# The first 4 KB of each row of w1 in loads of 2 to 32 rows

## The chip, the core and the metric

The kernel runs on one NeuronCore of a Trainium2 chip; the other seven are idle. The metric is the device time of one execution in microseconds (us), as the median of several runs. Five engines work side by side: PE (TensorE, the matrix multiplications), DVE (VectorE), ACT (ScalarE), POOL (GpSimd) and SP (SyncE, which here does nothing but start transfers). They meet at semaphores only. Transfers between the memory (HBM) and the on-chip buffer (SBUF, 128 partitions, called rows below) are carried by 16 DMA engines. An instruction on SP or ACT issues a transfer, and the profile counts the transfers of each issuer as one queue. A transfer raises a semaphore by 16 in all once its data has arrived.

## The reference

One token goes through a parallel block: the sum of the input, attention over a cache of 65536 positions, and a small MLP. All numbers are 32-bit floats.

```python
xn = layernorm(x)                                   # x: 512 numbers
q  = (xn @ wq) as 32 heads of 128                   # wq: 512 x 4096
k, v: 8 heads of 65536 x 128, each used by 4 query heads
scores = einsum("bhqd,bhkd->bhqk", q, k) * 128 ** -0.5
o  = einsum("bhqk,bhkd->bhqd", softmax(scores), v)
attention = o (32 * 128 numbers) @ wo               # wo: 4096 x 512
mlp = relu(xn @ w1) @ w2                            # w1: 512 x 1792, w2: 1792 x 512
y  = x + attention + mlp                            # 512 numbers
```

The keys and the values are 256 MiB each; wq and wo are 8 MiB each, w1 and w2 3.5 MiB each. So 561 MB have to come in, and 2 KB go out.

## The kernel before

**Stages.** SBUF has two large tiles, `kt` and `vt`, of 128 rows by 16384 numbers (64 KB of each row, 8 MiB in all), and a tile `wt` of 128 rows by 7168 numbers (28 KB of each row, 3.5 MiB). First `wq` comes into `kt` in three loads (of 16, 16 and 32 KB of each row), then `w1` into `wt` in one load. Then come the cache's pieces in turn: 32 loads of keys into `kt` and 32 of values into `vt`, each of 128 rows with 64 KB, alternating. At the end `wo` comes into `kt` in three loads and `w2` into `wt` in five, of 12, 8, 4, 2 and 2 KB of each row (`W2_CUTS`). All of these loads are issued by SP, on one queue.

**What sets the order.** Everything is written out by hand. SP issues the three loads of wq and that of w1 with nothing in their way. A load of keys waits for the semaphore `kfree`, that is, until the scores of the keys before have left `kt` and their largest has been found; a load of values waits for `vfree`, until PE has multiplied the values before. So at most one load is in flight and one more queued behind it.

**What the engines do.** For each piece of keys PE computes scores against four queries (L313), DVE transposes them (L366) and finds the largest, ACT takes the exponentials (L256), and PE multiplies them with the values (L292). Between the two, PE runs matrix multiplications over the MLP's first layer, three times over (`PASSES`, L281); the first of them waits for the semaphore `sum`.

**The use of w1.** POOL waits until all of w1 is in (L217), multiplies its four parts of 1792 numbers by the normed input (L219) and adds the four up (L222 to L224). The last addition raises `sum`. `wt` is next written when w2 comes at the very end.

**The end.** SP issues w2's five loads once POOL has the MLP's hidden layer (L226). PE multiplies each part of w2 as it arrives (L331, then L339 for the last three loads), DVE transposes the sum (L417), and SP stores the result (L179).

Of the kernel before, what the change touches and what calls it, by code (L numbers as in the profile page):

```python
# [12 lines left out]
P = 128  # L13
D = 512
# [15 lines left out]
FB = DFF_ALL // P  # L30
# [13 lines left out]
W2_CUTS = [6, 4, 2, 1, 1]  # L44
W2_SUM = 12
W2_ROWS = 10
PASSES = 3


def take(e, sem, n=1):  # L50

    return e.sem_inc(sem, -n).wait_op(sem, n, "sem-ge")  # L52
# [7 lines left out]
def attention_and_mlp_kernel(  # L60
# [12 lines left out]
    sp, pe, dve, act, pool = nc.sync, nc.tensor, nc.vector, nc.scalar, nc.gpsimd  # L73
    scale = float(DH) ** -0.5

    def sbuf(name, *shape):
        return nc.alloc_sbuf_tensor(name, list(shape), F32).ap()
# [3 lines left out]
    def sem(name):  # L81
        if name not in sems:
            sems[name] = nc.alloc_semaphore(name)
        return sems[name]
# [7 lines left out]
    wt = sbuf("wt", P, FB * D)  # L92
# [47 lines left out]
    w1_row = w1.rearrange("p a f -> p (a f)")  # L140
# [16 lines left out]
    for i in range(1, len(WQ_CUTS)):  # L157
        cut = slice(wq_at[i], wq_at[i + 1])
        sp.dma_start(kt[:, cut], wq_row[:, cut]).then_inc(sem(WQ_SEMS[i]), 16)  # L159
    sp.dma_start(wt, w1_row).then_inc(sem("w1"), 16)  # L160
    take(sp, sem("kfree"))
    sp.dma_start(kt, k[0, 0]).then_inc(sem("k"), 16)
    with sp.Fori(0, NCH - 1) as n:
# [7 lines left out]
    for i in range(len(WO_CUTS)):  # L171
        cut = slice(wo_at[i] * D, wo_at[i + 1] * D)
        sp.dma_start(kt[:, cut], wo_row[:, cut]).then_inc(sem(f"wo{i}" if i else "k"), 16)
    sp.wait_ge(sem("hT"), 1)
    for i in range(len(W2_CUTS)):
        cut = slice(w2_at[i] * D, w2_at[i + 1] * D)
# [37 lines left out]
    after(pool.tensor_copy(qpad[:, :XA], xn), "pool", chain[0]).then_inc(sem("q"), 1)  # L214
    f = DFF_ALL
    w1_of = [wt[:, a * f : (a + 1) * f] for a in range(XA)]
    pool.wait_ge(sem("w1"), 16)  # L217
    for a in range(XA):
        last = pool.tensor_scalar_mul(w1_of[a], w1_of[a], xn[:, a : a + 1])  # L219
    last.then_inc(sem("pool"), 1)  # L220
# [50 lines left out]
    with nc.body("turns", valid_engines=[pe.engine]):  # L271
# [3 lines left out]
        with pe.If(t > 1):  # L275
            after(pe.transpose(pma[:GROUP, :P], m, ident), "d2p").then_inc(sem("p2d"), 1)  # L276
            after(pe.matmul(pmb[:, :GROUP], ones[:GROUP, :], dg, start=True, stop=True), "d2p", 2).then_inc(sem("p2d"), 1)  # L277

            with pe.Fori(0, PASSES):
                for c in range(CT):  # L280
# [8 lines left out]
            for i in range(n):  # L289
                c = 32 * (i % CT)  # L290
                b = i * WIDE
# [32 lines left out]

    for b in range(W2_ROWS):
        if b == w2_at[1]:
# [4 lines left out]
        last = pe.matmul(  # L331
            y4[c : c + 1, :], hT[:, b : b + 1], wt[:, b * D : (b + 1) * D], start=(b < CT), stop=(b >= W2_ROWS - CT)
        )
        if b in w2_at:
            after(last, f"w2{w2_at.index(b)}", 16)
    last.then_inc(sem("p2d"), 1)
    for b in range(W2_ROWS, FB):
        for c in range(CT):
            last = pe.matmul(  # L339
                yacc[32 * c : 32 * c + 1, :], hT[:, b : b + 1], wt[:, b * D + c * P : b * D + (c + 1) * P],  # L340
                start=(b == W2_ROWS), stop=(b == FB - 1),
            )
# [113 lines left out]
```

## Time and profile before

| what | value |
|---|---|
| time, median of 3 runs | 1303.13 us (1302.83 to 1303.29) |
| span of the profiled execution | 1301.3 us |
| bytes moved | 561.02 MB, 431 GB/s over the span |
| share of the 16 DMA engines taken by SP's queue | 99.7% |
| PE busy | 774.9 us (60%) |
| DVE busy | 274.8 us (21%) |
| ACT busy, POOL busy | 76.2 us, 34.8 us |
| w1's load, issue to landing | 28.9 us |

The span reaches from the first to the last instruction of the profiled execution; it is the only time that this execution has. The runs that were timed lie 1.8 us above it. A row of the timeline has the start in us, the duration in us, the engine with the line of the kernel, the operation with what it writes and reads, and in brackets how long the engine was idle before it and what ended that. SPq is a DMA being issued by SP, PEld a weight load of PE. A row of a table by stretches has the stretch, its length, the busy time of each engine with its instructions, the clock granted to TensorE, the busy share of the DMA engines and the rate.

### The profile page before, as it was taken

The numbers are of one execution on the slowest core, as the hardware profiler recorded it, in microseconds if no ns is written. First come the engines' busy times: TensorE is split into PE (matmuls) and PEld (weight loads), VectorE is DVE, ScalarE is ACT, GpSimd is POOL, SyncE is SP. The second block draws the span as 40 slices with busy tenths as digits, with TensorE's granted clock in tenths as the row PEclk, the third lists the DMA queues.
The fourth block names the chain that finished last, engine by engine and source line by source line (L and its number), as shares of the span: only waits on it lengthen the run. The fifth ranks groups of instructions, "written<-read, shape, count | busy, mean of one in ns | idle before, by whom it ended". The sixth has DMA issues, their size and how long they took to land.

```text
span 1301.3 us, 13055 instructions
## 1 busy us (share of the span) xinstructions
PE 774.9 (60%) x5474; PEld 231.1 (18%) x5474; DVE 274.8 (21%) x466; ACT 76.2 (6%) x299; POOL 34.8 (3%) x30
## 2 busy tenths in 40 slices
PE   3365674665576456566555566666567466557557
PEld 1111121111121111121111121111112111112112
DVE  2211222211222220222220122221122221122222
ACT  1000000000000000000000000000000000000000
POOL 1900000000000000000000000000000000000000
PEclk9677877776887777786776777677777777777779
DMA  9999999999999999999999999999999999999998
GB/s 403 451 419 451 419 451 419 435 435 419 451 419 451 419 451 419 449 421 423 447 419 451 419 451 419 451 419 435 435 419 451 419 451 419 451 419 443 427 420 370
DMA packets 11236, 561.02 MB, mean 431 GB/s; under 512 B 1505, under 2 KB 1505, under 8 KB 1890
## 3 DMA queue, kind: packets, MB, share of 16 engines
q1 hardware_dynamic: 11088, 561.00, 99.7%
q10 hardware_dynamic: 146, 0.00, 0.0%
q8 instruction: 1, 0.02, 0.0%
q14 instruction: 1, 0.01, 0.0%
HBM read 560.99 MB, written 0.00 MB: 431 GB/s over the span
## 4 chain that ended last, share of the span: by engine, by line
issue 94%; DMA 3%; POOL 2%; SPq 0%; PE 0%; DVE 0%; POOLq 0%
DMA wt<-w 3%; POOL wt L219 1%; POOL wt L224 0%; POOL wt L222 0%; POOL wt L223 0%; SPq L177 0%; SPq L159 0%; PE banks L339 0%; DVE ysb L417 0%; SPq L151 0%; POOL hT L226 0%; SPq L452 0%; POOLq L156 0%
## 5 line engine op out<-in xcount | busy, mean ns | idle before, releaser
L313 PE MATMUL banks<-kt,qpad 128*32 128x512 f32 x2176 | 310.0, 733 | 311.1 <-PEq L52 308.7
L292 PE MATMUL banks<-vt,probs 128*16 128x512 f32 x2048 | 271.3, 690 | 82.1 <-PEq L52 82.1
L366 DVE STREAM_TRANSPOSE tr<-banks 128x1024 f32<-128x1024 f32 x136 | 170.0, 1250 | 471.4 <-PE banks L313 466.8
L313 PEld LDWEIGHTS banks<-kt,qpad 128*32 128x32 f32 x2176 | 84.5, 131 | 509.6 <-issue 496.3
L281 PE MATMUL banks<-wt,ones 128*1 128x448 f32 x768 | 121.3, 786 | 0.0
L292 PEld LDWEIGHTS banks<-vt,probs 128*16 128x16 f32 x2048 | 68.4, 108 | 298.4 <-issue 298.4
L392 DVE COPY o_sb<-banks 128x512 f32<-128x512 f32 x32 | 22.1, 692 | 455.3 <-PE banks L292 455.3
L254 ACT ACTIVATE corr<-diff 128x8 f32<-128x8 f32 x32 | 6.7, 208 | 1179.8 <-ACTq L52 1179.8
L256 ACT ACTIVATE probs<-tr,nb_new 128x128 f32<-128x128 f32 x128 | 65.3, 521 | 0.0
L276 PE MATMUL banks<-ident,m 128*4 128x128 f32 x32 | 9.7, 303 | 78.9 <-DVE m L384 78.9
L302 PE MATMUL banks<-sel,o_sb 128*128 128x4 f32 x256 | 32.8, 252 | 18.7 <-PEq L52 18.7
L302 PEld LDWEIGHTS banks<-sel,o_sb 128*128 128x128 f32 x256 | 31.0, 191 | 20.6 <-issue 20.6
L226 POOL TENSOR_SCALAR hT<-ysum 128x14 f32<-128x14 f32 x1 | 0.3, 257 | 1220.7 <-DVE ysum L404 1220.7
L384 DVE TENSOR_REDUCE m<-tr 128x4 f32<-128x512 f32 x32 | 32.2, 1006 | 2.9
L281 PEld LDWEIGHTS banks<-wt,ones 128*1 128x1 f32 x768 | 20.2, 100 | 58.9 <-issue 58.4
L277 PE MATMUL banks<-dg,ones 4*128 4x4 f32 x64 | 15.4, 309 | 20.0 <-DVE dg L387 20.0
L256 ACT ACTIVATION_READ_ACCUMULATOR probs<-tr,nb_new 128x1 f32 x128 | 24.0, 187 | 0.0
L276 PEld LDWEIGHTS banks<-ident,m 128*4 128x4 f32 x32 | 2.6, 81 | 108.0 <-DVE m L384 108.0
L219 POOL TENSOR_SCALAR wt<-wt,xn 128x1792 f32<-128x1792 f32 x4 | 19.1, 4797 | 16.5 <-DMA wt<-w 16.5
L277 PEld LDWEIGHTS banks<-dg,ones 4*128 4x128 f32 x64 | 12.6, 245 | 27.1 <-DVE dg L387 27.1
L299 PEld LDWEIGHTS banks<-part_sum,ones 128*128 128x128 f32 x64 | 9.5, 188 | 27.2 <-issue 27.2
L395 DVE TENSOR_TENSOR lo_run<-lo_run,banks 128x8 f32<-128x8 f32 x32 | 5.2, 163 | 40.0 <-DVEq L52 40.0
(69 smaller groups left out, 91.1 us busy)
## 6 DMA issues: line engine op xcount, KB each, us to landing
kt<-wq SPq DMA_DIRECT2D x2, 2048.0 KB, 9.3
kt<-wq SPq DMA_DIRECT2D x1, 4096.0 KB, 20.8
kt<-wo SPq DMA_DIRECT2D x1, 4096.0 KB, 15.5
kt<-wo SPq DMA_DIRECT2D x2, 2048.0 KB, 22.2
wt<-w SPq DMA_DIRECT2D x1, 3584.0 KB, 28.9
wt<-w SPq DMA_DIRECT2D x1, 1536.0 KB, 9.5
wt<-w SPq DMA_DIRECT2D x1, 1024.0 KB, 11.7
kt<-k SPq DMA_DIRECT2D x32, 24.1
```

Of the source, the lines that this page charges most:

```text
L219: last = pool.tensor_scalar_mul(w1_of[a], w1_of[a], xn[:, a : a + 1])
L256: last = act.activation(probs[:, :, g], tr[:, :, g], AF.Exp, bias=nb_new[:, g : g + 1], scale=scale, accum_out=part_sum[:, g : g + 1],)
L276: after(pe.transpose(pma[:GROUP, :P], m, ident), "d2p").then_inc(sem("p2d"), 1)
L277: after(pe.matmul(pmb[:, :GROUP], ones[:GROUP, :], dg, start=True, stop=True), "d2p", 2).then_inc(sem("p2d"), 1)
L281: ins = pe.matmul(hrow[32 * c : 32 * c + 1, :], ones[:, :1], hb[:, :, 32 * c : 32 * c + 32], start=True, stop=True,)
L292: last = pe.matmul(acc[c : c + WIDE * GROUP, :], probs[:, b : b + WIDE, :].rearrange("p b g -> p (b g)"), vt[:, b * DH : (b + WIDE) * DH], ...
L299: pe.matmul(lo_new[:, 0, :], ones, part_sum, start=True, stop=True).then_inc(sem("vfree"), 1)
L302: last = pe.matmul(lo_new[:, 1, :], o_sb[:, b, :], sel[:, b, :], start=(b == 0), stop=(b == WIDE - 1),)
L313: last = pe.matmul(pair[s // 2 % 2][32 * c : 32 * c + 32, s % 2 * 512 : s % 2 * 512 + 512], qpad, kb[:, s * 16 : s * 16 + 16, c, :], start ...
L366: ins = after(dve.transpose(tr2[:, s * 1024 : (s + 1) * 1024], pair[s % 2]), "p2d", s + 1)
L384: dve.reduce_max(m, tr.rearrange("p b i -> p i b")[:, :GROUP, :], axis=AX.X).then_inc(sem("d2p"), 1)
L392: after(dve.tensor_copy(o_sb.rearrange("p b d -> p (b d)"), acc), "p2d", 7).then_inc(sem("d2p"), 1)
```

## The change

The one load of w1 becomes eleven. The first 4 KB of each row (1024 of its 7168 numbers) come in ten loads (the change is announced as twelve; the list of cuts makes ten), each for some of the rows alone: rows 0 to 13, 14 and 15, 64 to 75, 76 to 79, 16 to 25, 26 to 31, 80 to 87, 88 to 95, 32 to 63, and 96 to 127, issued in this order. The other 24 KB of each row come in one load of all 128 rows. All eleven raise the semaphore `w1`, and POOL waits for the sum of their counts, so that it starts when the last of them is in.

```diff
+W1_STEP = 1024
+W1_ROWS = [(0, 14, 16), (64, 76, 80), (16, 26, 32), (80, 88, 96), (32, 64), (96, 128)]
...
-    sp.dma_start(wt, w1_row).then_inc(sem("w1"), 16)
+    w1_loads = [(slice(a, b), slice(0, W1_STEP)) for rows in W1_ROWS for a, b in zip(rows, rows[1:])]
+    w1_loads.append((slice(0, P), slice(W1_STEP, FB * D)))
+    for rows, cut in w1_loads:
+        sp.dma_start(wt[rows, cut], w1_row[rows, cut]).then_inc(sem("w1"), 16)
     take(sp, sem("kfree"))
...
-    pool.wait_ge(sem("w1"), 16)
+    pool.wait_ge(sem("w1"), 16 * len(w1_loads))
     for a in range(XA):
         last = pool.tensor_scalar_mul(w1_of[a], w1_of[a], xn[:, a : a + 1])
```

On SP, between the last load of wq and the first load of keys, one row stood for w1 (`wt` is the tile of w1, `kt` that of wq and of the keys; behind the names stand the rows and the numbers of each). Before:

```order
L151 DMA kt<-wq 128x4096
L452 UNCONDITIONAL_BRANCH
L159 DMA kt<-wq 128x4096
L159 DMA kt<-wq 128x8192
L160 DMA wt<-w 128x7168
L162 DMA kt<-k 128x16384
```

The same place on SP in the changed kernel:

```order
L161 DMA kt<-wq 128x8192
L165 DMA wt<-w 14x1024
L165 DMA wt<-w 2x1024
L165 DMA wt<-w 12x1024
L165 DMA wt<-w 4x1024
L165 DMA wt<-w 10x1024
L165 DMA wt<-w 6x1024
L165 DMA wt<-w 8x1024 x2
L165 DMA wt<-w 32x1024 x2
L165 DMA wt<-w 128x6144
L167 DMA kt<-k 128x16384
```

Ten narrow loads now stand ahead of a wide one that is shorter by what they carry, and the first load of keys has moved behind them; nothing else on SP has moved, and the other engines have the same rows in the same order.

## The prediction

> **What bounds the kernel now.** I read the page's slices and its queue table first, then the table by stretches, then the timeline at the three places where a transfer releases an engine.
>
> The page's slices and its third part:
>
> ```profile
> DMA  9999999999999999999999999999999999999998
> DMA packets 11236, 561.02 MB, mean 431 GB/s; under 512 B 1505, under 2 KB 1505, under 8 KB 1890
> ...
> q1 hardware_dynamic: 11088, 561.00, 99.7%
> ```
>
> The DMA engines are busy in every slice, and SP's queue alone takes 99.7% of what sixteen engines have. The table by stretches says where the small rest lies:
>
> ```profile
> 0.00:31.00 31.00, 9.98 (x68) 3.28 (x68) 9.34 (x9) 4.61 (x11) 3.51 (x22) 0.96 1.01 423
> 31.00:1250.00 1219.00, 729.05 (x5115) 217.44 (x5115) 249.31 (x431) 69.33 (x279) 31.05 (x7) 0.75 1.00 434
> ```
>
> In the 1219 us of keys and values the DMA share is 1.00 at 434 GB/s, while PE is busy for 729 us of it. So this is sixteen pipes that never stop; whatever a pipe gets to do beside its bytes moves everything behind it, up to the end.
>
> How even the pipes run is seen where PE begins on keys that have just landed, for the first and the last piece of keys:
>
> ```profile
> 50.77 9.48 PE L313 MATMUL banks<-kt,qpad 128*32 128x512 f32 x64 [24.50 <-PEq L52]
> ...
> 1250.46 8.68 PE L313 MATMUL banks<-kt,qpad 128*32 128x512 f32 x64 [7.62 <-PEq L52]
> ```
>
> Between them lie 31 loads of keys and 31 of values: (1250.46 - 50.77) / 62 = 19.350 us for 8 MiB. An engine has 8 of the 128 rows, so a row of 64 KB takes it 19.350 / 8 = 2.419 us.
>
> What small rows cost is seen at the end, where PE waits for each part of w2 in turn (1536, 1024, 512, 256 and 256 KB):
>
> ```profile
> 1292.94 0.11 PEld L331 LDWEIGHTS banks<-wt,hT 128*1 128x1 f32 x8 [2.54 <-DMA wt<-w]
> ...
> 1295.44 0.16 PEld L331 LDWEIGHTS banks<-wt,hT 128*1 128x1 f32 x8 [0.70 <-DMA wt<-w]
> 1296.72 0.32 PEld L339 LDWEIGHTS banks<-wt,hT 128*1 128x1 f32 x16 [1.12 <-DMA wt<-w]
> ...
> 1298.02 0.10 PEld L339 LDWEIGHTS banks<-wt,hT 128*1 128x1 f32 x8 [0.36 <-DMA wt<-w]
> ```
>
> The third part is 128 rows of 4 KB, just the bytes that the change cuts out of w1: 1296.72 - 1295.44 = 1.28 us, or 0.160 us for a row of 4 KB on one engine. The last two parts carry as much again in two loads: 1298.02 - 1296.72 = 1.30 us, so one more load with eight more rows per engine cost 0.02 us. From 2.419 us for 64 KB and 0.160 us for 4 KB, 60 KB cost 2.259 us, so 4 KB of pure transfer is 0.151 us and 0.009 us is paid per row whatever its length.
>
> **The change, part by part.**
>
> *Eleven issues for one on SP.* SP issues the loads of wq and w1 at the start, and then has nothing to do until the first keys:
>
> ```profile
> 1.34 0.83 SPq L159 DMA_DIRECT2D kt<-wq  x2
> 2.22 0.69 SPq L160 DMA_DIRECT2D wt<-w  x1
> 26.46 0.33 SPq L162 DMA_DIRECT2D kt<-k  x1
> ...
> 22.66 1.25 DVE L366 STREAM_TRANSPOSE tr<-banks 128x1024 f32<-128x1024 f32 x1 [2.90 <-DMA kt<-wq]
> ```
>
> At the dearest issue there, 0.69 us, eleven take 7.6 us and the last is out at 2.22 + 7.6 = 9.8 us. The DMA engines are on wq until shortly before 22.66 us, where DVE is released by its last load, so the issues are covered by some 12 us, and SP is back at its wait for `kfree` long before 26.46 us. I cost them at nothing; if a narrow load took over 1.8 us to issue, the pipes would run dry at w1. No other queue is passed: SP's own rows behind are the loads of keys and values, which wait for other things.
>
> *The bytes of w1.* They stay 3.5 MiB. Cutting each row in two costs each engine eight times 0.009 us, 0.07 us, inside the 0.2 us of the next step.
>
> *Ten narrow loads in place of 1.28 us of even work.* This is the term that decides. Before, each engine has eight 4 KB pieces here. A load of n rows that are not split can use n engines at most. I assume that a load gives its rows out in equal shares from the first engine on: then 14 rows go one each to fourteen engines, 2 rows to the first two, and so on, and the two loads of 32 give two rows to each. The first two engines get 8 + 4 = 12 pieces and the last two get 4, with a ramp between. The first take 12 x 0.160 = 1.92 us, 0.64 us over the even share; the last take 0.64 us. So the engines come to the keys up to 1.28 us apart. Ten loads more on the busiest engine, at 0.02 us each, are 0.2 us. Sum: +0.84 us on the engine that is last.
>
> Nothing takes this back. Every later load has eight equal rows for each engine, and a load is only there when its last engine is. The ends of this term: nothing, if the engine that gets most was ahead of the others by that much, which no view shows; and, if each of the eight narrow loads went to one and the same engine, 64 + 4 rows x 0.160 = 10.9 us in place of 1.28, +9.6 us. I take 0.84 us, since the row of the 512 KB part is the same bytes, and because the busy share of 1.00 shows all sixteen sharing a load of 128 rows evenly.
>
> [...] No row here shows a load of fewer than 128 rows in `wt`.
>
> *POOL's longer wait.* POOL starts on w1 when all of it is in, and behind it stands PE's first multiplication over the sum:
>
> ```profile
> 31.17 19.12 POOL L219 TENSOR_SCALAR wt<-wt,xn 128x1792 f32<-128x1792 f32 x4 [16.46 <-DMA wt<-w]
> ...
> 58.39 3.99 POOL L224 TENSOR_TENSOR wt<-wt 128x1792 f32<-128x1792 f32 x1
> ...
> 64.23 4.66 PE L281 MATMUL banks<-wt,ones 128*1 128x448 f32 x24
> 69.91 7.06 PE L292 MATMUL banks<-vt,probs 128*16 128x512 f32 x64 [1.02 <-PEq L52]
> ```
>
> POOL is done at 58.39 + 3.99 = 62.38 us, PE starts at 64.23 us: 1.85 us of room, and the keys that PE waits for come later by as much as w1 does. Behind L281 PE was idle for another 1.02 us before the values landed. Nothing.
>
> *Are the pipes still fed?* SP issues the next keys while the values of the turn are still coming; the first such issue, and one late in the run (there the loads of wo, which take the place of keys, against the landing of the values at 1269.82):
>
> ```profile
> 65.47 0.34 SPq L167 DMA_DIRECT2D kt<-k  x1
> ...
> 1263.90 1.29 SPq L173 DMA_DIRECT2D kt<-wo  x3
> ...
> 1269.82 9.22 PE L292 MATMUL banks<-vt,probs 128*16 128x512 f32 x64 [3.45 <-PEq L52]
> ```
>
> The issue comes 69.91 - 65.47 = 4.4 us before the slowest engine is through at the start and 5.9 us late in the run. An engine 1.3 us ahead still has 3 us. And an engine that did run dry would only lose its lead.
>
> *The end.* The store is issued at a fixed distance behind the last landing:
>
> ```profile
> 1298.92 0.34 SPq L179 DMA_DIRECT2D y<-ysb  x1
> ```
>
> It stands 0.9 us behind the last part of w2 and moves with it.
>
> Sum: 1301.3 + 0.84 = 1302.1 us for the profiled execution. The median, 1303.13 us, lies 1.8 us above its span for what lies around it, so I forecast 1304.0 us.
>
> **The rivals.** About 0.2%, 2.6 us, is what a measurement of this kernel can tell from no change: below 1300.5 us is faster, above 1305.7 us slower.
>
> *Engines that write to neighbouring rows share one engine's rate.* Before, no two engines are seen to hinder each other: 434 GB/s at a share of 1.00. But in the narrow loads rows that one engine used to have are given to several at once. Say four rows that lie together can take in what one engine carries. Then a pair of narrow loads, 16 rows side by side, takes 4 x 0.160 = 0.64 us instead of 0.16, and a load of 32 rows, two rows for each engine with two engines at the same place, 0.64 us too. Four pairs and two loads of 32 make six times 0.64 = 3.84 us against 1.28: +2.56 us, with the 0.2 us of the ten loads 1305.9 us. If the groups overlap two by two, since rows below 64 and above alternate, it is 1.92 us and, with 0.2 us, the 1304.0 us of the forecast again. If the uneven shares (0.64 us) come on top and late narrow rows meet the wide load of engines that are ahead, it is 1306.5 us and more, to 1307.3 us. It decides from the point at which the groups don't overlap. For it: no row excludes it, as no load of before puts two engines so close. Against it: no row shows one engine slowing another, and whether pieces as short as 0.16 us meet at all depends on how far apart the engines stand.
>
> [...]
>
> *Engines out of step run faster.* If the 0.009 us per row is paid because all sixteen change rows together, spreading them saves up to that on each of 64 x 8 rows of keys and values: 512 x 0.009 = 4.6 us, less 0.84: 1299.4 us. It counts as faster from three quarters of the 4.6 us on. Against it: the part of w2 with rows of 8 KB took 1295.44 - 1292.94 = 2.50 us, 0.312 us per row, which is 2 x 0.151 us and 0.010 us more; so the price is the same for rows of 4, 8 and 64 KB and looks fixed. A third of it would give 1302.4 us.
>
> *The narrow loads use few engines, or one.* Then the far end above holds, 1303.1 + 9.6 = 1312.7 us. Against it: the loads of 128 rows use all sixteen evenly, and a rule that leaves fourteen rows to one engine is the farthest from that.
>
> *The change does nothing.* If every narrow load were spread over all engines, the ramp would be missing and only the 0.2 us remain: 1303.3 us. It counts with the forecast.
>
> **How the numbers follow.** The forecast with the last rival, from 1303.2 to 1304.4 us: 0.45. Sharing: 0.40, of which 0.27 lies above 1305.7 us. Out of step: 0.12, of which 0.03 is below 1300.5 us. Few engines: 0.03, slower. So faster 0.03, slower 0.27 + 0.03 = 0.30, within 0.2% 0.67. The range leaves out the better half of "out of step" (0.06) and the upper end of sharing with the few engines (0.11): 1302.3 to 1306.9 us.
>
> **What would show it.** In the profile after: the rows of w1's issues on SP end before 12 us (issues hidden). PE's first L313 on keys, at 50.77 us before, stands at 51.6 us by the forecast, at 53.3 us or later by sharing, and POOL's L219 moves by as much. The step between loads stays at 19.35 us; below 19.34 us the engines gain by being out of step. The distance from the last load of keys to the store stays as it is. The prediction is wrong if the first L313 on keys moves by over 2 us, if the step between loads changes by over 0.02 us (62 of them are 1.2 us), or if SP's issues reach 20 us.

## The result and the profile after

| | before | after |
|---|---|---|
| time, median | 1303.21 us (9 runs, 1302.83 to 1303.95) | 1306.59 us (9 runs, 1306.09 to 1307.72) |
| span of the profiled execution | 1301.3 us | 1304.5 us |
| first multiplication on keys starts | 50.77 us | 53.59 us |
| last part of w2 is used | 1298.02 us | 1300.74 us |
| the store is issued | 1298.92 us | 1301.65 us |
| the store, issue to landing | 1.4 us | 2.0 us |

The ratio is 1.0027 with a 95% interval from 1.0018 to 1.0036: 3.4 us slower.

The page's lines on the DMA engines, of the kernel after:

```profile
DMA  9999999999999999999999999999999999999998
...
DMA packets 11460, 561.02 MB, mean 430 GB/s; under 512 B 1601, under 2 KB 1601, under 8 KB 2114
...
q1 hardware_dynamic: 11312, 561.00, 99.7%
```

The busy share is what it was, 99.7%, and so are the bytes. The loss can't be seen in the share. It is seen in the rate, in the table by stretches, from 22 to 29 us, where most of w1 comes in. Before:

```profile
22.00:29.00 7.00, 3.64 (x32) 0.96 (x32) 4.29 (x5) 0.00 (x0) 0.00 (x0) 0.95 0.99 422
```

The same stretch after, and the stretch of keys and values behind it:

```profile
22.00:29.00 7.00, 3.64 (x32) 0.96 (x32) 4.26 (x5) 0.00 (x0) 0.00 (x0) 1.00 1.08 322
...
31.00:1250.00 1219.00, 723.17 (x5115) 216.43 (x5115) 249.30 (x431) 69.54 (x279) 31.05 (x7) 0.75 1.00 434
```

The engines are as busy (the last but one number) and move a quarter less (the last). That is a sign of the loss and not its size: a share above 1 shows that a stretch is also credited with what ends behind it, and w1 goes on behind 29 us. The size comes from the trace's records of single pieces (a piece is one row's part of a load, carried by one engine). The pieces of w1 took an engine 8.57 us in the mean before and 10.76 us after, 2.19 us more. The sixteen engines then came to the first keys within 0.4 us of each other before and within 1.4 us after, and the last one was 0.7 us behind their mean instead of 0.2 us. So some 2.2 us are slower pieces and some 0.5 us are uneven engines. From 31 us to 1250 us the rate is 434 GB/s, as before.

SP, DVE, POOL and PE in the timeline of after:

```profile
2.22 4.42 SPq L165 DMA_DIRECT2D wt<-w  x11
...
23.02 1.25 DVE L371 STREAM_TRANSPOSE tr<-banks 128x1024 f32<-128x1024 f32 x1 [2.99 <-DMA kt<-wq]
...
34.01 19.12 POOL L224 TENSOR_SCALAR wt<-wt,xn 128x1792 f32<-128x1792 f32 x4 [19.22 <-DMA wt<-w]
...
53.59 8.51 PE L318 MATMUL banks<-kt,qpad 128*32 128x512 f32 x64 [26.97 <-PEq L54]
...
1253.24 9.43 PE L318 MATMUL banks<-kt,qpad 128*32 128x512 f32 x64 [8.57 <-PEq L54]
```

SP has issued the eleven loads by 2.22 + 4.42 = 6.6 us. All of w1 is in 34.01 - 31.17 = 2.84 us later than before, and the first keys 53.59 - 50.77 = 2.82 us. From there to the last keys nothing more is lost: (1253.24 - 53.59) / 62 = 19.349 us per load, against 19.350 us. A small part of the delay shows ahead of w1: DVE's wait for the last load of wq ends at 23.02 us instead of 22.66 us, though that load is issued ahead of the narrow ones (23.04 and 22.70 us in the repetitions of both kernels below). Why was not found.

The end of after:

```profile
1300.74 0.10 PEld L344 LDWEIGHTS banks<-wt,hT 128*1 128x1 f32 x8 [0.33 <-DMA wt<-w]
...
1301.65 0.34 SPq L184 DMA_DIRECT2D y<-ysb  x1
```

The store is issued 2.73 us later than before. The table of transfers has its time from issue to landing, first of the kernel before:

```profile
y<-ysb SPq DMA_DIRECT2D x1, 2.0 KB, 1.4
```

and of the kernel after:

```profile
y<-ysb SPq DMA_DIRECT2D x1, 2.0 KB, 2.0
```

So 0.6 us more are lost at the very end: 2.73 + 0.6 = 3.3 us, against 3.4 us in the medians.

### The profile page after: what moved, and what is told of

Its sections match the earlier page's. It is cut to its first block, busy times and chain, and to the rows that moved or that the text cites. A ratio compares the mean times of both kernels' runs of the same rounds, so it can differ in the third digit from the quotient of the medians.

```text
span 1304.5 us, 13065 instructions
## 1 busy us (share of the span) xinstructions
PE 772.1 (59%) x5474; PEld 230.9 (18%) x5474; DVE 274.8 (21%) x466; ACT 76.4 (6%) x299; POOL 34.8 (3%) x30
## 2 busy tenths in 40 slices
DMA packets 11460, 561.02 MB, mean 430 GB/s; under 512 B 1601, under 2 KB 1601, under 8 KB 2114
## 3 DMA queue, kind: packets, MB, share of 16 engines
q1 hardware_dynamic: 11312, 561.00, 99.7%
## 4 chain that ended last, share of the span: by engine, by line
issue 93%; DMA 3%; POOL 2%; SPq 0%; PE 0%; DVE 0%; POOLq 0%
DMA wt<-w 3%; POOL wt L224 1%; POOL wt L227 0%; POOL wt L228 0%; POOL wt L229 0%; SPq L165 0%; PE banks L344 0%; SPq L161 0%; SPq L182 0%; DVE ysb L422 0%; PE banks L357 0%; SPq L153 0%; POOL hT L231 0%; SPq L457 0%; POOLq L158 0%
## 5 line engine op out<-in xcount | busy, mean ns | idle before, releaser
L371 DVE STREAM_TRANSPOSE tr<-banks 128x1024 f32<-128x1024 f32 x136 | 170.0, 1250 | 472.9 <-PE banks L318 468.8
L224 POOL TENSOR_SCALAR wt<-wt,xn 128x1792 f32<-128x1792 f32 x4 | 19.1, 4797 | 19.2 <-DMA wt<-w 19.2
```

The source lines that it names most:

```text
L371: ins = after(dve.transpose(tr2[:, s * 1024 : (s + 1) * 1024], pair[s % 2]), "p2d", s + 1)
```

## The experiments

Two theories stood against each other. **Sharing**: engines that write at the same time to rows lying together share what one engine otherwise has. **Uneven shares and a price per load**: only the number of pieces on the busiest engine counts, and each narrow load costs something by itself; to reach 3.4 us it would be 0.64 us and ten times 0.27 us. The marker is the start of PE's first multiplication on keys; it is free of what happens at the end. In all the kernels a row of `wt` is filled from the same row of w1 in memory, so no run tells whether the engines meet where they write or where they read. All kernels compute everything. The edits are to the changed kernel.

### The same loads with their rows apart

```diff
-W1_ROWS = [(0, 14, 16), (64, 76, 80), (16, 26, 32), (80, 88, 96), (32, 64), (96, 128)]
+W1_ROWS = [(0, 14, 16), (64, 12, 16), (1, 10, 16), (65, 8, 16)]
...
-    w1_loads = [(slice(a, b), slice(0, W1_STEP)) for rows in W1_ROWS for a, b in zip(rows, rows[1:])]
+    w1_loads = []
+    for at, n, of in W1_ROWS:
+        w1_loads.append((slice(at, at + 4 * n - 3, 4), slice(0, W1_STEP)))
+        w1_loads.append((slice(at + 4 * n, at + 4 * of - 3, 4), slice(0, W1_STEP)))
+    w1_loads += [(slice(a, P, 4), slice(0, W1_STEP)) for a in (2, 3)]
```

> The ten narrow loads keep their sizes (14, 2, 12, 4, 10, 6, 8, 8, 32, 32 rows of 4 KB), so every engine gets as many pieces as in the changed kernel, but the rows of a load lie four apart instead of side by side. Marker: the start of PE's first multiplication on keys, 50.77 us before and 53.59 us after the change. Sharing (engines that write to rows lying together share one engine's rate): the first engines no longer meet four at a place but two, so four pairs at 2 x 0.16 us and two loads of 32 at 0.64 us, 2.6 us against 1.28 us, with uneven shares between +0.9 and +2.1 us: marker 51.7 to 52.9 us, time 1304.1 to 1305.3 us. Uneven shares and a price per load (0.64 us, and 0.27 us for each of ten loads to make up the 3.4 us measured): nothing changes, marker 53.6 us, time 1306.6 us.

Measured: 1304.84 us, ratio 1.0014 (1.0005 to 1.0024). The marker in this kernel's timeline:

```profile
52.19 9.31 PE L322 MATMUL banks<-kt,qpad 128*32 128x512 f32 x64 [25.73 <-PEq L54]
```

and, in the table of transfers, its store:

```profile
y<-ysb SPq DMA_DIRECT2D x1, 2.0 KB, 2.1
```

The marker moved by 1.42 us instead of 2.82, with loads of the same sizes in the same number. Half of the loss hangs on which rows a load takes together. Uneven shares and a price per load can't explain that: by the records the last engine is 0.65 us behind the mean of the sixteen here and 0.69 us in the changed kernel, while the mean itself is 1.4 us earlier.

### Eleven loads of all rows

```diff
-    w1_loads = [(slice(a, b), slice(0, W1_STEP)) for rows in W1_ROWS for a, b in zip(rows, rows[1:])]
-    w1_loads.append((slice(0, P), slice(W1_STEP, FB * D)))
+    at = [640 * i for i in range(11)] + [FB * D]
+    w1_loads = [(slice(0, P), slice(a, b)) for a, b in zip(at, at[1:])]
```

> w1 comes in eleven loads too, but each has all 128 rows: ten of 2.5 KB and one of 3 KB of each row. Count and issue as in the changed kernel, shares even, no rows given to another engine. Sharing: only the fixed price, 80 more rows per engine at 0.009 us at most, +0.2 to +0.9 us: marker 51.0 to 51.7 us, time 1303.4 to 1304.1 us. A price per load: ten times 0.27 us, marker 53.5 us, time 1305.9 us.

Measured: 1303.97 us, ratio 1.0006 (0.9997 to 1.0016); the marker stands at 51.54 us:

```profile
51.54 9.63 PE L318 MATMUL banks<-kt,qpad 128*32 128x512 f32 x64 [25.18 <-PEq L54]
```

That is +0.77 us for 80 more rows on each engine, 0.0096 us per row, just the price worked out from w2 and the keys. The number of loads itself costs next to nothing: beside 80 x 0.009 = 0.72 us, ten loads leave 0.05 us. In the changed kernel, with the shares that the prediction assumed, the busiest engine has only some twelve rows more than before, 0.1 us.

### Sixteen loads of eight rows, apart and together

Four rows apart:

```diff
+W1_ROWS = [0, 64, 32, 96]
...
+    w1_loads = [(slice(a + i, a + i + 29, 4), slice(0, W1_STEP)) for i in range(4) for a in W1_ROWS]
```

> The first 4 KB of each row come in sixteen loads of 8 rows that lie four apart, so that eight engines have 16 pieces each and eight have none, and no two of a load write to rows lying together. Sharing: uneven shares alone, 16 x 0.16 - 1.28 = +1.28 us, and 0.3 us for sixteen loads, +1.6 us; up to +2.7 us if the last pieces meet the wide load of the engines that are ahead. Marker 52.4 to 53.5 us, time 1304.7 to 1305.8 us. A price of 0.27 us per load: 1.28 + 4.3 = +5.6 us, marker 56.4 us, time 1308.8 us. If the engines out of step by 2.6 us ran faster, the step between loads would fall below 19.34 us.

Side by side:

```diff
+W1_ROWS = [0, 64, 32, 96]
...
+    w1_loads = [(slice(a + 8 * i, a + 8 * i + 8), slice(0, W1_STEP)) for i in range(4) for a in W1_ROWS]
```

> As the kernel with sixteen loads of 8 rows four apart, with the same counts on the same engines, but the 8 rows of a load lie side by side. Sharing: four engines at a place, sixteen times 0.64 us = 10.2 us against 1.28 us, +9 us if the groups don't overlap, +4 us if two of them (low and high rows) go side by side: marker 54.8 to 59.7 us, time 1307 to 1312 us. Uneven shares and a price per load: the same time as with rows four apart.

Measured: 1306.66 us apart, ratio 1.0028 (1.0018 to 1.0039), and 1309.38 us together, ratio 1.0049 (1.0033 to 1.0066). The marker apart:

```profile
53.75 9.10 PE L318 MATMUL banks<-kt,qpad 128*32 128x512 f32 x64 [27.07 <-PEq L54]
...
1253.24 8.40 PE L318 MATMUL banks<-kt,qpad 128*32 128x512 f32 x64 [7.90 <-PEq L54]
```

and together:

```profile
55.96 8.64 PE L318 MATMUL banks<-kt,qpad 128*32 128x512 f32 x64 [29.13 <-PEq L54]
```

With loads of the same sizes, rows side by side cost 55.96 - 53.75 = 2.21 us more. In both kernels the records show two groups of eight engines that come to the keys over 2 us apart, so the counts are alike and the difference is in the speed. Sharing is confirmed in kind, not in the size assumed: a 4 KB row took 0.362 us in the median (the middle value) with rows together, 2.3 times the 0.16 us of w2 and not four times; it took 0.238 us with rows apart and 0.302 us in the changed kernel. Apart, the marker moved by 2.98 us, a little more than the 2.7 us allowed for. A likely reason, which no run tests, is that the eight engines with nothing here go on to their 24 KB rows at once, among the rows that the other eight still carry; the first 4 KB rows of this kernel took 0.159 us, and later ones 0.24 us. The step between loads, (1253.24 - 53.75) / 62 = 19.347 us, shows no gain worth the name from engines out of step: 62 x 0.003 = 0.2 us against the kernel before.

### Even shares, rows side by side

```diff
+W1_ROWS = [(0, 32), (64, 96), (32, 64), (96, 128)]
```

> The first 4 KB of each row come in four loads of 32 rows side by side (0 to 31, 64 to 95, 32 to 63, 96 to 127), two rows for each engine in each: no uneven shares, and only four loads more. Sharing: two engines at a place, four times 0.64 us = 2.56 us against 1.28 us, +1.3 us, or +0.5 us where low and high rows overlap: marker 51.3 to 52.1 us, time 1303.7 to 1304.5 us. Uneven shares alone: +0.1 us, marker 50.9 us, time 1303.3 us.

Measured: 1305.62 us, ratio 1.0019 (1.0009 to 1.0028). The marker:

```profile
51.70 9.41 PE L318 MATMUL banks<-kt,qpad 128*32 128x512 f32 x64 [25.17 <-PEq L54]
```

and, in the table of transfers, its store:

```profile
y<-ysb SPq DMA_DIRECT2D x1, 2.0 KB, 2.7
```

The marker moved by 0.93 us without uneven shares (the engines come to the keys within 0.3 us of each other): sharing costs by itself. But the time rose by 2.3 us, more than twice that. The store, at 2.7 us instead of 1.4, has 1.3 us of the rest.

### 127 rows and one

```diff
+W1_ROWS = [(0, 127, 128)]
```

> The first 4 KB of each row come in one load of 127 rows and one of the last row. If a load uses the largest number of engines up to 16 that divides its rows, 127 rows go to one engine, which then has 128 pieces of 0.16 us, 20.5 us against 1.28 us: +19.2 us, marker 70 us, time 1322.4 us. If a load's rows were given out as evenly as can be to sixteen engines: +0.1 us, marker 50.9 us, time 1303.3 us.

Measured: 1332.66 us, ratio 1.0220 (1.0203 to 1.0238). The first and the last keys:

```profile
78.70 9.18 PE L318 MATMUL banks<-kt,qpad 128*32 128x512 f32 x64 [52.00 <-PEq L54]
...
1284.38 8.79 PE L318 MATMUL banks<-kt,qpad 128*32 128x512 f32 x64 [11.10 <-PEq L54]
```

The marker moved by 27.9 us: a load of 127 rows does run on one engine. The page counts 1507 packets under 512 B here, two more than before for two loads more, where ten more loads of 128 rows made 160 more (1665); and the share of the DMA engines, below, falls to a sixteenth. The delay is 8.7 us over the 19.2 us expected for 128 pieces of 0.16 us. The records give the 128 pieces 0.227 us in the mean, 29.1 us in all against 1.28 us of even work, so the marker's delay is the one engine. Its first fifty rows, while it was alone, took 0.159 us each. Soon after the other fifteen had begun their rows of 24 KB, it needed 0.36, 0.35, 0.20 and 0.25 us for the first to the fourth row of each group of four (means over rows 64 to 123, if it takes them in order). So engines do slow one another, and the pattern fits places of four rows.

The table by stretches of this kernel:

```profile
22.00:29.00 7.00, 3.64 (x32) 0.96 (x32) 4.19 (x5) 0.00 (x0) 0.00 (x0) 1.00 0.06 24
...
61.00:100.00 39.00, 14.39 (x103) 4.20 (x107) 7.01 (x10) 2.29 (x9) 29.13 (x7) 0.68 0.70 294
```

From 22 to 29 us the share is 0.06, a sixteenth: one engine at work, and fifteen idle, since SP was still issuing (see the end of this text). The share is low once more behind 61 us, and the step between loads is (1284.38 - 78.70) / 62 = 19.446 us, so 6 us more are lost behind the marker. This execution was the longest of the four, 1337.13 us, and lost more than the median shows.

### Three times the bytes

```diff
-W1_STEP = 1024
+W1_STEP = 3072
```

> The changed kernel with 12 KB of each row in the ten narrow loads instead of 4 KB, so each piece is three times as long (4 KB cost 0.151 us and 0.009 us per row, so 0.46 us) and the number of loads is the same. Sharing: six groups of 4 x 0.46 us = 11 us against 3.7 us, +7.4 us, up to +9.2 us with the uneven shares; at the least three times the 2.8 us that the marker moved by, +8.5 us: marker 58 to 60 us, time 1310.5 to 1312.3 us. Uneven shares and a price per load: 1.85 + 2.7 = +4.6 us, marker 55.4 us, time 1307.7 us.

Measured: 1317.96 us, ratio 1.0118 (1.0101 to 1.0134). The marker:

```profile
64.09 8.90 PE L318 MATMUL banks<-kt,qpad 128*32 128x512 f32 x64 [35.16 <-PEq L54]
```

The marker moved by 13.3 us, far beyond the 4.6 us of a price per load. It is beyond the 7.2 to 9.2 us that sharing allowed as well, and 4.7 times the 2.8 us of 4 KB pieces instead of three times. So the loss grows with the bytes, but not in proportion. The records say the same: a 12 KB row took 1.36 us in the mean, 2.9 times the 0.464 us of w2's rows of 12 KB, and a 4 KB row of the changed kernel 0.292 us, 1.8 times 0.162 us. A line through both points, 5.25 us per 4 KB, meets zero at pieces of 1.9 KB; that is a reading of two points, and no run shows why longer pieces lose more than in proportion.

### Another order of the same loads

```diff
+W1_ROWS = [(0, 14, 16), (16, 26, 32), (32, 64), (64, 76, 80), (80, 88, 96), (96, 128)]
```

> The ten narrow loads of the changed kernel in another order: those of rows 0 to 63 first, then those of rows 64 to 127, instead of in turn. Each engine's pieces are the same. Sharing with groups that overlap: low and high rows no longer go side by side, up to 1.3 us later than the changed kernel, marker 53.6 to 54.9 us. Uneven shares and a price per load: the same as the changed kernel, marker 53.6 us, time 1306.6 us.

Measured: 1307.05 us, ratio 1.0028 (1.0017 to 1.0038); marker 53.84 us, 0.25 us behind the changed kernel and 0.20 us behind its repetition below. Whether the alternating order of low and high rows saved anything can't be told from this.

### Is the late store chance?

The late store stands in no term of the prediction, and in no expectation so far. Three kernels were run as they were, beside one new one, in which the four loads of 32 rows carry 512 bytes of each row instead of 4 KB:

```diff
-W1_STEP = 1024
+W1_STEP = 128
...
+W1_ROWS = [(0, 32), (64, 96), (32, 64), (96, 128)]
```

> The kernel before, unchanged, as a control beside the next three. What is in question is the last store (2 KB), which took 1.4 us from issue to landing before, 2.0 us after the change, 2.7 us with four loads of 32 rows and 1.4 us again with eleven loads of 128 rows. If narrow loads make it late, it is 1.4 us here, as in the profile of before, and the time 1303.2 us. If it is late by chance, or by where a program happens to lie, it may be 2.0 us or more here, and the time 1303.8 us or more.

> The changed kernel, unchanged, beside the same control. If narrow loads make the store late: 2.0 us again, time 1306.6 us. If chance or place does: 1.4 us is as likely, and the time is then 1306.0 us, 2.8 us over the kernel before, which is what the marker moved by.

> The eleven loads of 128 rows once more. If narrow loads make the store late: 1.4 us again, time 1304.0 us. If chance or place does: 2.0 us or more is as likely, and the time then over 1304.4 us.

> The four loads of 32 rows side by side, with 512 bytes of each row instead of 4 KB. Sharing has an eighth of the bytes to act on, so the keys' marker moves by 0.1 to 0.2 us, 50.9 us. If the mere presence of narrow loads makes the store late: 2.0 to 2.7 us for the store, time 1304.0 to 1304.6 us. If the store's delay comes from sharing, or from chance: 1.4 us for the store and 1303.3 us.

| kernel | time, median | ratio (95%) | marker moved by | store, issue to landing |
|---|---|---|---|---|
| before | 1303.08 us | 0.9999 (0.9989 to 1.0009) | 0.0 us | 1.4 us |
| the change | 1306.99 us | 1.0029 (1.0017 to 1.0040) | 2.9 us | 2.2 us |
| eleven loads of all rows | 1304.01 us | 1.0005 (0.9995 to 1.0015) | 0.85 us | 1.4 us |
| 512 bytes in loads of 32 rows | 1304.29 us | 1.0008 (0.9999 to 1.0018) | 0.4 us | 2.5 us |

The last one's marker:

```profile
51.14 9.71 PE L318 MATMUL banks<-kt,qpad 128*32 128x512 f32 x64 [24.55 <-PEq L54]
```

and, in the table of transfers, its store:

```profile
y<-ysb SPq DMA_DIRECT2D x1, 2.0 KB, 2.5
```

With an eighth of the bytes the marker moved by 0.4 us, twice what was expected; DVE's wait for wq ends 0.3 us later here (22.98 us), so little of it is w1. The store is late all the same, by 1.1 us, though it is issued almost 1.3 ms after these loads. So it is not chance, and it doesn't go with the bytes. In fourteen profiles the store took 1.4 us in all those whose loads either had all 128 rows (before, twice; eleven loads of all rows, twice) or put the narrow ones on one engine (127 rows and one), and 2.0 to 2.7 us in the nine with loads of 2 to 32 rows over several engines. What it is that lasts to the end was not found.

## Why the prediction was right and wrong

**The time lay in the range; the case called likeliest was the wrong one.** The measured 1306.6 us falls to the rival that had 0.40: engines that write to neighbouring rows share one engine's rate. The range held because it took in most of that rival. The sign that the prediction named for being wrong, over 2 us at the first keys, did come: 2.82 us.

**The step that failed** is the term for the ten narrow loads. The prediction put +0.84 us there, from 1.28 us of 4 KB rows in w2, and took the value of the nearest row: the same bytes in the same time. The bytes are the same, the time is not: by the records the rows of that part of w2 took 0.16 us each, those of the narrow loads 0.16 to 0.49 us, 0.29 us in the mean, and the 24 KB rows behind them were slowed too (1.05 us in the mean, 0.91 us the fastest). In its place stand 2.82 us at the marker. The parts that the runs show: slower pieces make some 2.2 us and uneven engines some 0.5 us, where the sum had nothing and 0.64 us; the price per row is right (0.0096 us against 0.009) and makes some 0.1 us here; rows four apart instead of side by side take 1.4 us off, so at least that much is sharing; and even shares with sharing cost 0.93 us in four loads of 32.

**The rival's own size.** It put the sum at 1305.9 to 1307.3 us and the marker at 53.3 us or later; 53.59 us came out. That the size came out is in part luck: 0.6 us of the time is the store, for which it has no term, and the 24 KB rows behind were slowed, which it has only for late narrow rows. Its term of 4 x 0.160 us is a supposition, that four rows lying together take in what one engine carries, and no run shows it: a 4 KB row was slowed 1.8 times in the mean in the changed kernel, and 2.3 times in the median with loads of 8 rows side by side. That the piece's length matters more than in proportion was not in it. In kind the runs agree with sharing: with counts equal, 8 rows side by side cost 2.21 us more than 8 rows four apart. That the meeting place is where rows are written was assumed; no run here separates it from where they are read. The weighing was at fault: nothing in the trace bore on two engines at one place, and the forecast took silence as a reason for no cost.

**The ramp.** That shares are equal from the first engine on, so that the busiest has 12 pieces, was assumed. What the runs show fits one engine for each row of a load of 2 to 14 rows. The page of after counts 96 packets under 512 B more than that of before (1601 against 1505), which is 14 + 2 + 12 + 4 + 10 + 6 + 8 + 8 + 16 + 16; ten more loads of 128 rows made 160 more (1665), four of 32 rows 64 (1569), and sixteen of 8 rows 128 (1633). Loads of 8 rows leave two groups of eight engines. But 127 rows ran on one engine, so shares are not always spread as evenly as can be. The engines come to the keys 1.4 us apart, against 1.28 us in the prediction; the share of each engine in the ten loads was not counted one by one, and no run shows that a load begins at the first engine.

**Issues hidden under wq.** Right: the last issue ends at 6.6 us, within the 9.8 us allowed.

**POOL's wait.** Right: POOL is 2.84 us later, the keys 2.82 us, and PE's step between loads didn't change.

**The pipes stay fed, and nothing is taken back.** Right: 19.349 us per load. With one engine 28 us behind the others (127 rows and one) it no longer holds: 19.446 us.

**Engines out of step run faster.** This rival, which had 0.12, did not come: the step is 19.349 us after the change and 19.347 us with eight engines far ahead, against 19.350 us.

**The end.** Half right. The store is issued 0.91 us behind the last part of w2, 0.90 us before. That its own duration would stay was taken for granted; it rose by 0.6 us, a fifth of the whole loss.

## What to carry to other kernels

Here, with the DMA engines busy all the time (99.7%), a load of few rows that lie side by side was not a cheaper load: several engines then worked on neighbouring rows at once, they stayed busy, and the rate fell (322 GB/s from 22 to 29 us, against 422 before). Four loads of 32 such rows cost 0.93 us at the marker, eleven loads of all 128 rows 0.77 us. Read the rate beside the share, stretch by stretch, and place the loss by the first instruction that waits for what comes next. When a price is taken from the nearest row of a profile, ask what that row has that the new work lacks; here it was a load of all 128 rows.

## What was not expected

- Loads of 2 to 32 rows at the start make the 2 KB store at the end land 0.6 to 1.3 us later. In nine of nine profiles with such loads on several engines it took 2.0 to 2.7 us, in five of five without them 1.4 us, and four loads of 512 bytes per row were enough. It is paid in runs without a profile too: with four loads of 32 rows the marker explains 0.9 us of the 2.3 us.
- SP can be held by issuing. Eleven narrow loads took it 4.4 us with rows side by side and 7.8 us with rows four apart, eleven loads of 128 rows 19.1 us, and three loads of which one had 127 rows 27.6 us. The rows of the last two kernels:

```profile
2.21 19.12 SPq L165 DMA_DIRECT2D wt<-w  x11
```

```profile
2.22 27.56 SPq L165 DMA_DIRECT2D wt<-w  x3
```

  Eleven loads of 128 rows were all issued at 21.3 us, ahead of the end of wq. With 127 rows and one the issuing ended at 29.8 us, behind it, and that is where fifteen engines stood idle. So an issue is not always the 0.4 us of SP's first one, and a cover of 12 us is less than it looks. What the issuing waits for was not found.
